# Chunked attention ahead of two expert layers: v loaded as one transfer per head, memory scored apart, q and k laid out six tokens to a partition

## The chip, the cores and the metric

One core of a Trainium2 chip runs the whole program. The metric is the device time of one execution in microseconds (us); lower is better. A run's time is that of the execution as a whole; the profile's span, from the first to the last instruction, is a little shorter.

## What is computed

Chunked attention with a few memory tokens for 4 batches and 8 heads, 768 tokens, head width 64, in float32; its output goes through a soft mixture of experts and then through a top-2 mixture of experts. Only the attention is touched:

```python
chunk, left_ctx, right_ctx = (32, 16, 8)
for c in range(nc):
    c_start = c * chunk
    c_end = c_start + chunk
    l_start = max(0, c_start - left_ctx)
    r_end = min(S, c_end + right_ctx)
    q_c = q[:, :, c_start:c_end]
    k_full = np.concatenate([mem_k, k[:, :, l_start:r_end]], axis=2)   # 8 memory tokens, up to 56 of context
    v_full = np.concatenate([mem_v, v[:, :, l_start:r_end]], axis=2)
    scores = scale * np.matmul(q_c, k_full.transpose(0, 1, 3, 2))
    a = softmax(scores)
    out[:, :, c_start:c_end] = np.matmul(a, v_full)
x = moe(out)          # soft mixture of 8 experts, 4 slots each
return moe2(x)        # top-2 mixture of 8 experts
```

## The kernel before

Attention works on units of one batch and two heads (16 units), and each unit in two halves of 12 chunks: 32 steps, counted by i or n in the code. The two heads of a unit stand on partitions 0 to 63 and 64 to 127. Tokens go in pairs of an even and an odd one (z is the parity), so that a row of 512 B in DRAM holds two tokens of one head.

- `load_raw` (L972) brings q or k of a unit on SP's DMA queue into RW, three buffers. In before, a partition gets six rows of 512 B: row p of each of the six groups of 128 token pairs.
- `tr` (L1024) makes six PE transposes (L1032) of a raw buffer into PSUM, and four ScalarE copies (L1041) bring them to QT (q, both parities interleaved) or into KB (k by head and parity). KB is KB_W wide: 20 columns for each chunk, 16 of k and 4 of memory's k.
- `fill_mem` (L1016) copies memory's k from mkT into those 4 columns of every chunk on GpSimd, four copies for a unit (in before from the loop, L1299).
- `load_v` (L983) fills one of four VB buffers with v of a half, head by head. Partition rows 0 to 15 and 20 to 31 of a head's 32 hold the context's token pairs of the 12 chunks, two transfers on SP's queue (`piece`, L992); rows 16 to 19 hold memory's v, one transfer on GpSimd's queue (L1003).
- `spread` (L1008) copies 32 partitions of VB, 768 columns, into the block for the other parity: head 0 on VectorE (L1014), head 1 on ScalarE (L1012).
- `qk` (L1045) computes a step's scores: 12 matmuls, one for each chunk, with 32 queries stationary and 4 x 32 columns of KB moving (two heads by two parities, each 28 of k and 4 of memory; the order of a head's 64 keys is free, as long as k and v have the same). Four chunks run side by side on 32 columns of the array each. A float32 matmul is two instructions in the trace.
- `mxr` and `sub` (L1068, L1074) on VectorE take the maximum and subtract it, `expo` (L1078) on ScalarE, `at` (L1083) three PE transposes, `atc` (L1089) a ScalarE copy, `av` (L1098) the product with VB, `nrm` (L1107 to L1110) the division on VectorE, `xt` and `xtc` a transpose of the result for the router's logits, `lg`, `lgc`, `lt`, `ltc` the logits.

The order is written out by hand. Step i of the loop (L1292) issues: qk(n), mxr(n) with n = i + 1, tr(i + 3), fill_mem, spread(n, 0), sub(n), expo(n), at(i), atc(i), spread(n, 1), av(i - 1), nrm(i - 1), load_v(i + 3), a weight piece in even steps (`load_piece`, 512 KB, SP's queue), the logits' parts in some steps, xt(i - 2), xtc(i - 2). Every engine runs its own instructions in this order. On VectorE, the spreading of v stands between a step's maximum and its subtraction. The last steps are spelled out in the list ORDER.

After attention, `soft` runs the first expert layer. Its weights come through the same SP queue: 16 pieces are loaded during attention, 16 into attention's buffers once these are free, the others as the layer frees buffers (`next_load`).

## Time and profile before

| | before |
|---|---|
| runs, us | 632.57 median of 3 (625.32 to 635.29) |
| the profiled execution's own time, us | 628.29 |
| its span, us | 626.5 |
| busy: PE, ACT, DVE, POOL, us | 500.8, 291.9, 332.8, 307.2 |
| DMA moved | 127.27 MB, 203 GB/s on average |
| mean granted TensorE clock | 0.926 |
| attention | about the first 185 us |

PE is TensorE, DVE VectorE, ACT ScalarE, POOL GpSimd, SP the engine that issues most transfers. The profile gives busy time by engine over stretches, waits (which engine stood still at which line, and what ended the wait), instructions in order of time, groups of instructions by line and shape, and the DMA queues with the rate over time. Averages over the whole span hide that the stages have different limits: attention and the soft layer in the first 260 us, the routing, and then the top-2 experts, where TensorE sets the end.

### The profile page before, as it was taken

Reading aid. Unit: us, or ns where it says so; the run is one execution under the profiler, and the core shown is the slowest. Engines: PE = TensorE matmul, PEld = TensorE weight load, DVE = VectorE, ACT = ScalarE, POOL = GpSimd, SP = SyncE. Lnnn points to the kernel's source line nnn. Section 1 sums busy time; section 2 is a strip of 40 time slices with the busy share of each in tenths; the row PEclk is TensorE's granted clock in tenths of the full one; section 3 lists DMA queues with packets and bytes.
Section 4 is the critical chain, followed back from the end, with each engine's and each line's share of the span. In section 5 each row is a group of like instructions: output and inputs, shape, how many; then the busy total and the mean of one; then the engine's idle time right before and its main releaser. Section 6 shows DMA issues by size and latency. Waiting matters only on the chain.

```text
span 626.5 us, 13927 instructions
## 1 busy us (share of the span) xinstructions
PE 500.8 (80%) x4667; PEld 272.6 (44%) x4667; DVE 332.8 (53%) x830; ACT 291.9 (47%) x510; POOL 307.2 (49%) x320
## 2 busy tenths in 40 slices
PE   3777767776787877437698989999999999979980
PEld 2555545554553332222353534545545445534530
DVE  5546574664776300669756475664747566452300
ACT  3867777775832110634352362634526263433310
POOL 6233333232202100069356576766758676877772
PEclk9979999888889998757898999999999999999995
DMA  9999999999999999974838779697987868435642
GB/s 149 192 204 211 189 224 181 248 194 185 219 275 374 377 410 415 290 264 169 251 41 265 181 152 237 163 248 173 235 230 184 204 156 207 80 71 95 95 57 34
DMA packets 116779, 127.27 MB, mean 203 GB/s; under 512 B 20128, under 2 KB 85300, under 8 KB 116708
## 3 DMA queue, kind: packets, MB, share of 16 engines
q1 hardware_dynamic: 97140, 109.30, 64.2%
q0 software_dynamic: 19152, 16.89, 20.2%
q8 instruction: 43, 0.70, 0.5%
q10 hardware_dynamic: 416, 0.15, 0.2%
q14 instruction: 28, 0.23, 0.1%
HBM read 94.84 MB, written 20.42 MB: 184 GB/s over the span
## 4 chain that ended last, share of the span: by engine, by line
PE 39%; DVE 6%; DMA 4%; ACT 3%; issue 2%; POOL 2%; SPq 0%; POOLq 0%; DVEq 0%; ACTq 0%
PE l L719 32%; PE l L685 3%; DMA out_dram<-y,idx 3%; PE g L340 2%; POOL out_dram L750 1%; DVE lo L695 1%; DMA C<-G 1%; ACT hi L687 1%; PE l L716 1%; DVE G L392 1%; DVE W L409 1%; ACT W L405 1%; DVE W L792 1%; ACT y L737 0%; DVE W L524 0%
## 5 line engine op out<-in xcount | busy, mean ns | idle before, releaser
L750 POOL DMA_INDIRECT out_dram<-y,idx x96 | 157.0, 1635 | 82.5 <-DMA out_dram<-y,idx 47.5
L719 PE MATMUL l<-W,hi 128*128 (+1 forms) x768 | 181.8, 391 | 0.4 <-ACT hi L687 0.4
L695 DVE SCALAR_TENSOR_TENSOR lo<-l,hi 128x1024 f16<-128x1024 f32 x49 | 59.9, 1223 | 111.8 <-ACT hi L687 97.6
L719 PEld LDWEIGHTS <-hi 128*128 128x128 f16 x768 | 75.1, 100 | 87.5 <-issue 11.8
L737 ACT ACTIVATE y<-l,gw 128x512 f32<-128x512 f32 x49 | 33.6, 685 | 155.8 <-PE l L719 76.4
L719 PE MATMUL l<-W,lo 128*128 (+1 forms) x384 | 92.5, 384 | 4.7 <-DVE lo L695 4.7
L1003 POOL DMA_DIRECT2D arena<-in_mem_v_dram x64 | 39.5, 619 | 101.2 <-PE av L1098 100.9
L644 POOL DMA_INDIRECT cg<-table,idx x49 | 52.1, 1063 | 19.9 <-issue 10.7
L719 PEld LDWEIGHTS <-lo 128*128 128x128 f16 x384 | 37.2, 99 | 49.7 <-DVE lo L695 5.5
L687 ACT ACTIVATE hi<-l 128x1024 f16<-128x1024 f32 x49 | 50.3, 1026 | 10.0 <-PE l L685 9.9
L1014 DVE COPY arena<-arena 32x768 f32<-32x768 f32 x32 | 18.1, 566 | 58.1 <-DMA arena<-in_v_dram 57.1
L409 DVE SCALAR_TENSOR_TENSOR W<-w,sc,W 128x1024 f16<-128x1024 f32 x31 | 42.3, 1390 | 0.2
L1055 PE MATMUL st<-arena,qT 128*32 128x128 f32 (+2 forms) x768 | 32.3, 309 | 12.5 <-ACT arena L1041 10.6
L1083 PE MATMUL at<-cf,a 128*128 128x128 f32 x96 | 18.2, 302 | 26.5 <-ACT aT L1089 25.4
L1032 PE MATMUL tr<-cf,arena 128*128 128x128 f32 x192 | 30.7, 300 | 10.8 <-DMA arena<-in_q_dram 9.9
L1041 ACT ACTIVATE qT<-tr 64x384 f32<-64x384 f32 x64 | 33.6, 526 | 8.6 <-PE tr L1032 7.4
L405 ACT ACTIVATE W<-w,sc 128x1024 f16<-128x1024 f32 x32 | 35.7, 1150 | 0.2
L1098 PE MATMUL av<-arena,aT 128*32 128x130 f32 x768 | 31.4, 295 | 4.4 <-issue 2.9
L1078 ACT ACTIVATE a<-a 128x384 f32<-128x384 f32 x32 | 16.7, 523 | 36.9 <-DVE a L1074 36.7
L1055 PEld LDWEIGHTS st<-arena,qT 128*32 128x32 f32 x768 | 23.5, 124 | 19.5 <-issue 16.0
L1041 ACT ACTIVATE arena<-tr 64x384 f32<-64x384 f32 x64 | 31.0, 484 | 2.1 <-PE tr L1032 1.3
L1032 PEld LDWEIGHTS tr<-cf,arena 128*128 128x128 f32 x192 | 22.4, 150 | 18.1 <-issue 10.2
(265 smaller groups left out, 678.0 us busy)
## 6 DMA issues: line engine op xcount, KB each, us to landing
w<-in_moe_w_dram SPq DMA_DIRECT2D x96, 512.0 KB
arena<-in_moe_w_dram SPq DMA_DIRECT2D x32, 512.0 KB
arena<-in_q_dram SPq DMA_DIRECT2D x16, 384.0 KB
arena<-in_k_dram SPq DMA_DIRECT2D x16, 384.0 KB
arena<-in_v_dram SPq DMA_DIRECT2D x63, 96.0 KB
out_dram<-zt SPq DMA_DIRECT2D x14, 384.0 KB
C<-G SPq DMA_DIRECT2D x21, 256.0 KB
CT<-G SPq DMA_DIRECT2D x21, 256.0 KB
```

The lines of the kernel that those rows point to most:

```text
L405: nc.scalar.activation(hi, w2, AF.Copy, scale=sc[:, rk, 5:6])
L409: stt(lo, w2, sc[:, rk, 5:6], hi, op0=OP.mult, op1=OP.subtract)
L644: nc.gpsimd.indirect_dma_start(out=CG[i], out_offset=None, in_=table, in_offset=bass.IndirectOffsetOnAxis(ap=idx[:, i:i + 1], axis=0))
L687: nc.scalar.activation(HI[i], p, AF.Relu)
L695: stt(LO[i].rearrange("p k t -> p (k t)"), p.rearrange("p k t -> p (k t)"), 0.0, HI[i].rearrange("p k t -> p (k t)"), op0=OP.max, op1=OP.s ...
L719: nc.tensor.matmul(P2[i], h[i][:, k, :], dyn(W2f, i, w * 4096 + 512 * k, 512, RG.get(i)), start=x == 0 and k == 0, stop=x == last and k == 7)
L737: nc.scalar.activation(YV[i], P2.pop(i), AF.Copy, scale=GW.pop(i))
L750: nc.gpsimd.indirect_dma_start(out=o, out_offset=bass.IndirectOffsetOnAxis(ap=idx[:, i:i + 1], axis=0), in_=y[:, DH * h:DH * h + DH], in_o ...
L1003: nc.gpsimd.dma_start(vcols(i, p + 16, 4, col, 128), bass.AP(tensor=mem_v.tensor, offset=mem_v.offset + (b * H + 2 * hp + h) * NMEM * D, a ...
L1032: nc.tensor.transpose(p[:, T, :], src[:, h, T, :], identf)
L1041: nc.scalar.activation(o, i, AF.Copy)
L1055: nc.tensor.matmul(st[32 * j:32 * j + 32, g, :, w0:w1], QT[u][:, 32 * c:32 * c + 32], kb[:, :, 20 * c + w0:20 * c + w1], start=True, stop= ...
```

## The change

For each head of a half, v's context is 28 consecutive partition rows, 0 to 27, and one transfer; memory's v goes to rows 28 to 31 (still from GpSimd's queue). The first and the last half have an edge chunk as a transfer of its own. KB holds k alone, 16 columns for each chunk; the scores of memory come from three matmuls a step with 128 queries stationary and the 16 columns of MK moving, which is filled once at the start; fill_mem and its copies are gone, and the 12 matmuls of a step move 4 x 28 columns. q and k come as six consecutive tokens (1,536 B) to a partition, in two rows; after the PE transposes the tokens are out of order, and the ScalarE copies put them in order by reading PSUM with a step of 128 elements inside a group of three.

```diff
--- before.py
+++ after.py
@@ -28,7 +28,7 @@
 F = 1024
 E = 8
 SL = 32
-KB_W = 20 * NCH + 12
+KB_W = 16 * NCH + 12
 VC = 194
 NEG = -1.0e30
 NTL = 60
@@ -958,7 +958,7 @@
     KB = [carve(4 * KB_W).rearrange("p (h z w) -> p h z w", h=2, z=2) for i in range(2)]
     RW = [carve(768).rearrange("p (h t e) -> p h t e", h=2, t=3) for i in range(3)]
     VB = [carve(NH * VC + D) for i in range(NV)]
-    mkT = carve(HP * B * NMEM).rearrange("p (c z b m) -> p c z b m", c=HP, z=2, b=B)
+    MK = carve(HP * B * 2 * NMEM).rearrange("p (c b h z m) -> p c b h z m", c=HP, b=B, h=2, z=2)
     XT = [wk.tile([128, 4, 384], F32, name=f"xT{z}", bufs=1) for z in range(2)]
     mkr = XT[0].rearrange("p j n -> p (j n)")[:H * NMEM, :B * 2 * D].rearrange("p (b z d) -> p b z d", b=B, z=2)
     one = wk.tile([128, 1], F32, name="one", bufs=1)
@@ -973,9 +973,9 @@
         u, x = divmod(n, 2)
         b, hp = divmod(u, HP)
         src = (q, k)[x]
-        nc.sync.dma_start(RW[n % 3].rearrange("p h t e -> p (h t) e"),
+        nc.sync.dma_start(RW[n % 3].rearrange("p h t e -> p h (t e)"),
                           bass.AP(tensor=src.tensor, offset=src.offset + (b * H + 2 * hp) * S * D,
-                                  ap=[[128, 128], [16384, 6], [1, 128]]))
+                                  ap=[[384, 128], [S * D, 2], [1, 384]]))
 
     def vcols(i, p, n, col, cols, c0=0, c1=NH):
         return custom(VB[i % NV][p:p + n], c0 * VC + col, [[VC, c1 - c0], [1, cols]])
@@ -994,13 +994,12 @@
                                   bass.AP(tensor=v.tensor, offset=o + first * 128 + a * 2048,
                                           ap=[[128, n], [2048, e - a], [1, 128]]))
 
-            piece(0, 16, -8, c0, NH)
+            piece(0, 28, -8, c0, c1)
             if c0:
-                piece(8, 8, 0, 0, 1)
-            piece(20, 12, 8, 0, c1)
+                piece(8, 20, 0, 0, 1)
             if c1 < NH:
-                piece(20, 8, 8, c1, NH)
-            nc.gpsimd.dma_start(vcols(i, p + 16, 4, col, 128),
+                piece(0, 24, -8, c1, NH)
+            nc.gpsimd.dma_start(vcols(i, p + 28, 4, col, 128),
                                 bass.AP(tensor=mem_v.tensor,
                                         offset=mem_v.offset + (b * H + 2 * hp + h) * NMEM * D,
                                         ap=[[128, 4], [0, NH], [1, 128]]))
@@ -1012,14 +1011,6 @@
             nc.scalar.activation(o, x, AF.Copy)
         else:
             nc.vector.tensor_copy(o, x)
-
-    def fill_mem(u, eng=nc.gpsimd):
-        b, hp = divmod(u, HP)
-        for h in range(2):
-            p = 64 * h
-            for z in range(2):
-                o = custom(KB[u % 2][p:p + 64, h, z, 16:], 0, [[20, NCH], [1, NMEM // 2]])
-                eng.tensor_copy(o, mkT[p:p + 64, hp, z, b:b + 1, :].to_broadcast([64, NCH, NMEM // 2]))
 
     def tr(n):
         u, x = divmod(n, 2)
@@ -1031,13 +1022,11 @@
             for T in range(3):
                 nc.tensor.transpose(p[:, T, :], src[:, h, T, :], identf)
             for r in range(2):
-                i = p[64 * r:64 * r + 64, :3].rearrange("p t a -> p (t a)")
+                i = custom(p[64 * r:64 * r + 64], 0, [[1, 128], [128, 3]])
                 if x == 0:
                     o = custom(QT[u][64 * h:64 * h + 64], r, [[2, 384]])
                 else:
-                    o = custom(KB[u % 2][64 * h:64 * h + 64, h, 1 - r if h == 0 else r, 8:], 0,
-                               [[20, NCH], [12, 2], [1, 8]])
-                    i = i.rearrange("p (c f a) -> p c f a", f=2, a=8)
+                    o = KB[u % 2][64 * h:64 * h + 64, h, 1 - r if h == 0 else r, 8:8 + S // 2]
                 nc.scalar.activation(o, i, AF.Copy)
         if n + 3 < 2 * NU:
             load_raw(n + 3)
@@ -1048,12 +1037,16 @@
         st = ps.tile([128, 3, 4, 32], F32, name="st", bufs=2)
         kb = KB[u % 2].rearrange("p h z w -> p (h z) w")
         for g in range(3):
+            t = 128 * (3 * s + g)
+            nc.tensor.matmul(st[:, g, :, 28:32], QT[u][:, t:t + 128], MK[:, hp, b].rearrange("p h z m -> p (h z) m"),
+                             start=True, stop=True)
+        for g in range(3):
             for j in range(4):
                 c = 12 * s + 4 * g + j
                 w0 = 8 if c == 0 else 0
-                w1 = 28 if c == NCH - 1 else 32
+                w1 = 24 if c == NCH - 1 else 28
                 nc.tensor.matmul(st[32 * j:32 * j + 32, g, :, w0:w1], QT[u][:, 32 * c:32 * c + 32],
-                                 kb[:, :, 20 * c + w0:20 * c + w1], start=True, stop=True,
+                                 kb[:, :, 16 * c + w0:16 * c + w1], start=True, stop=True,
                                  tile_position=(0, 32 * j))
         ST[i] = st
 
@@ -1062,7 +1055,7 @@
         if s == 0:
             nc.vector.memset(ST[i][0:32, 0, :, 0:8], NEG)
         else:
-            nc.vector.memset(ST[i][96:128, 2, :, 28:32], NEG)
+            nc.vector.memset(ST[i][96:128, 2, :, 24:28], NEG)
         st = ST[i].rearrange("p g (h z) w -> p (g h) (z w)", z=2)
         mx = wk.tile([128, 6], F32, name="mx")
         nc.vector.tensor_reduce(mx, st, AX.X, OP.max)
@@ -1257,6 +1250,7 @@
     nc.vector.memset(VB[0][0:32, 0:128], 0.0)
     for i in range(2):
         nc.gpsimd.memset(KB[0][64 * i:64 * i + 64, 1 - i], 0.0)
+    nc.gpsimd.memset(MK, 0.0)
     load_v(0)
     clear(0, nc.vector)
     load_raw(2)
@@ -1272,11 +1266,9 @@
         nc.tensor.transpose(p[:, b].rearrange("p c h m z -> p (c h m z)"), mkr[:, b], identf[:H * NMEM, :H * NMEM])
     for h in range(2):
         for z in range(2):
-            nc.vector.tensor_copy(mkT[64 * h:64 * h + 64, :, 1 - z if h == 0 else z].rearrange("p c b m -> p b c m"),
+            nc.vector.tensor_copy(MK[64 * h:64 * h + 64, :, :, h, 1 - z if h == 0 else z].rearrange("p c b m -> p b c m"),
                                   p[64 * h:64 * h + 64, :, :, h, :, z])
     tr(1)
-    fill_mem(0, nc.vector)
-    fill_mem(1)
     tr(2)
     load_v(2)
     nc.gpsimd.memset(one, 1.0)
@@ -1295,8 +1287,6 @@
         qk(n)
         mxr(n)
         tr(i + 3)
-        if s == 1:
-            fill_mem(u + 2)
         if i == 6:
             nc.gpsimd.dma_start(phis, phi.rearrange("(j p) s -> p j s", p=128))
         spread(n, 0)
```

## Rows read from the trace of the kernel before

**Rows 1.** Stretch, us; busy PE, PEld, DVE, ACT, POOL; clock; DMA share; GB/s.

```profile
18.00:172.00 154.00, 112.25 (x1779) 80.05 (x1774) 89.93 (x235) 114.41 (x209) 49.47 (x113) 0.92 1.11 205
```

**Rows 2.** Instructions in time: start, us, operation; exps 1, 15, 16 and 29.

```profile
18.97 0.52 ACT L1078 ACTIVATE a<-a 128x384 f32<-128x384 f32 x1 [0.48 <-DVE a L1074]
...
89.98 0.52 ACT L1078 ACTIVATE a<-a 128x384 f32<-128x384 f32 x1 [1.30 <-DVE a L1074]
93.91 0.52 ACT L1078 ACTIVATE a<-a 128x384 f32<-128x384 f32 x1
...
167.18 0.52 ACT L1078 ACTIVATE a<-a 128x384 f32<-128x384 f32 x1 [2.18 <-DVE a L1074]
```

**Rows 3.** Waits, 0 to 200 us: who waited for whom, us, times, longest.

```profile
DVE arena L1014 <- DMA arena<-in_v_dram: 57.1, 26, 4.5
ACT a L1078 <- DVE a L1074: 36.7, 24, 3.6
...
PE st L1055 <- ACT arena L1041: 10.6, 10, 1.4
```

**Rows 4.** DMA views of 2.6 to 5.6 (40 slices), 11.5 to 14.8, 185 to 195.

```profile
GB/s 26 51 142 278 306 355 340 341 341 348 355 348 348 341 355 341 348 355 348 328 335 348 355 341 321 300 287 294 294 277 345 270 249 280 287 283 294 335 290 438
...
DMA packets 791, 0.37 MB, mean 112 GB/s; under 512 B 99, under 2 KB 785, under 8 KB 791
...
DMA packets 1632, 4.10 MB, mean 410 GB/s; under 512 B 126, under 2 KB 126, under 8 KB 1630
```

**Rows 5.** DMA issues, 0 to 215 us: line, count, KB each.

```profile
w<-in_moe_w_dram SPq DMA_DIRECT2D x30, 512.0 KB
...
arena<-in_v_dram SPq DMA_DIRECT2D x63, 96.0 KB
arena<-in_v_dram SPq DMA_DIRECT2D x63, 72.0 KB
```

**Rows 6.** Groups by line, 0 to 200 us, ScalarE: busy us, mean ns | idle before.

```profile
L1041 ACT ACTIVATE qT<-tr 64x384 f32<-64x384 f32 x64 | 33.6, 526 | 8.6 <-PE tr L1032 7.4
...
L1041 ACT ACTIVATE arena<-tr 64x384 f32<-64x384 f32 x64 | 31.0, 484 | 2.1 <-PE tr L1032 1.3
...
L1012 ACT ACTIVATE arena<-arena 32x768 f32<-32x768 f32 x32 | 26.9, 842 | 2.9 <-DMA arena<-in_v_dram 2.2
...
L1078 ACT ACTIVATE a<-a 128x384 f32<-128x384 f32 x32 | 16.7, 523 | 36.9 <-DVE a L1074 36.7
L1089 ACT ACTIVATE aT<-at 128x384 f32<-128x384 f32 x32 | 15.7, 491 | 3.3 <-PE at L1083 2.6
```

**Rows 7.** The same view, VectorE's reads of PSUM.

```profile
L1068 DVE TENSOR_REDUCE mx<-st 128x6 f32<-128x384 f32 x32 | 17.9, 558 | 1.1
...
L1152 DVE TENSOR_REDUCE L<-xt 128x96 f32<-128x384 f32 x8 | 4.4, 550 | 0.3 <-PE xt L1147 0.3
```

**Rows 8.** Instructions in time on TensorE, a stretch almost without waits.

```profile
162.97 0.49 PE L1083 MATMUL at<-cf,a 128*128 128x128 f32 x3
...
163.39 0.87 PE L1098 MATMUL av<-arena,aT 128*32 128x130 f32 x24
...
164.08 0.83 PE L1135 MATMUL xt<-xT,phis 128*32 128x384 f32 x8
...
164.84 0.55 PE L1121 MATMUL xt<-cf,xs 128*128 128x128 f32 x3
...
165.32 0.86 PE L1055 MATMUL st<-arena,qT 128*32 128x128 f32 x24
...
166.11 0.87 PE L1032 MATMUL tr<-cf,arena 128*128 128x128 f32 x6
```

**Rows 9.** The same view, matmuls with 128 stationary and 32 moving columns.

```profile
197.86 1.12 PE L1241 MATMUL sm<-W,xT 128*128 128x32 f32 x8 [0.20 <-DVE W L1236]
```

**Rows 10.** The same view: the end of attention, VectorE and SP's queue.

```profile
182.19 0.55 DVE L1014 COPY arena<-arena 32x768 f32<-32x768 f32 x1 [2.19 <-DMA arena<-in_v_dram]
...
201.29 16.36 SPq L146 DMA_DIRECT2D w<-in_moe_w_dram  x16
```

## The prediction

> **What bounds the kernel now.** The stage to read is attention; the change touches nothing behind it. I read first the busy times over its steady part: from 18 to 172 us the DMA engines are busy all the time (share 1.11, packets overlapping) and yet move only 205 GB/s; ScalarE is busy 114.41 of 154 us, TensorE 112.25, VectorE 89.93, GpSimd 49.47 [rows 1]. Then the length of a step: one exp (L1078) runs per step, and from its 1st to its 29th the starts are 18.97 and 167.18, so 28 steps take 148.2 us, 5.29 us each [rows 2]. One step, from 89.98 to 93.91, took 3.93 us [rows 2]: the engines can turn faster than they do. Then the waits: VectorE stands 57.1 us in front of L1014, the spreading of v, for v's transfer; what VectorE has queued behind it, the subtraction, is then late for ScalarE's exp (36.7 us) [rows 3]. So v's landing sets the step.
>
> Why does v land late when its bytes are few? The DMA rates by stretch tell it. From 2.6 to 5.6 us, at the start, q and k are alone and run at 341 to 355 GB/s, in rows of 512 B; from 11.5 to 14.8 us mostly v and memory's v run, in rows of 512 B as well, at 112 GB/s; from 185 to 195 us weights run at 410 [rows 4]. So the row's length is not what makes v slow. It differs from q and k in that a transfer goes to 16 or to 12 partitions, not to 128. A step moves one q or k transfer (128 partitions x 6 x 512 B, 384 KB), v as 2 x (96 + 72) KB and half a weight piece of 512 KB [rows 5], memory's v (2 x 4 partitions x 12 x 512 B, 48 KB) and, on average, as much of zeros for the output. At those rates, in thousands of bytes: 393/341 = 1.15 us; (344 + 49)/112 = 3.51; 262/410 = 0.64; 49/341 = 0.14. The sum is 5.44 us against the 5.29 measured: the step is DMA time, and two thirds of it is v.
>
> **v as one transfer of 28 partitions.** Same rows and bytes, two transfers a step instead of four, 28 partitions reached at once instead of 16 and then 12. No row shows 28 partitions. Below: no gain, v stays at 112 GB/s. Above: 341, the 128-partition rate. If the rate goes with the partitions reached (14 on average gave 112), 28 give 224, and this is the row it is nearest to. Memory's v keeps its four partitions and, at 112, its 0.44 us; v's 344 KB go from 3.07 to 1.54 us. I take 1.6. The two fewer issues a step on SP, which has queued behind them only further loads, I cost at nothing: SP's queue is not what the waits name.
>
> [...]
>
> **q and k with rows of 1,536 B.** The same bytes in a third of the rows: between 341 (no gain) and 410 GB/s (weights, with longer rows) [rows 4]. I take 400, 0.98 us instead of 1.15.
>
> DMA after: 0.98 + 1.6 + 0.44 + 0.64 + 0.14 = 3.80 us a step. That is under what the engines need, so look who is next.
>
> **ScalarE.** A step has four copies of L1041 (526 ns for q, 484 for k), L1012 842, L1078 523, L1089 491: 2.02 + 1.86 = 3.88 us [rows 6], near the 3.93 of the fastest step. The change makes the four copies read PSUM with a step of 128 elements where they read it in a row. No ScalarE row shows that. The nearest is VectorE's L1152, which reads PSUM with a step of 32: 550 ns for 384 elements, against 558 for L1068 in a row [rows 7]. I cost it at nothing; it is the second rival.
>
> **TensorE.** From start to start in a stretch without waits: at 0.42, av 0.69, lg 0.76, xt 0.48, qk 0.79 us; tr, at most 0.87, about 0.70 [rows 8]. Each step has at, av, xt, qk and tr, 3.08 us; lg, and lt which is like xt, come every fourth step, 0.31 on average. The new part is three matmuls on the memory, with 128 stationary columns and 16 moving ones, in two passes each. The nearest row is L1241, 128 stationary and 32 moving: eight passes in 1.12 us, 0.14 each [rows 9]; so at most 6 x 0.14 = 0.84 us. Nothing at the least: every other step TensorE waits for k's copies ahead of qk, 10.6 us in 10 times [rows 3], and the memory's scores need only q, whose copies are a step older. I take 0.7. The narrower matmuls (112 columns for 128) give back at most an eighth of 0.79, 0.1. TensorE after: 3.08 + 0.31 + 0.7 - 0.1 = 3.99 us at full clock; granted was 0.92 on average, with more idle time than will be left [rows 1].
>
> **The rest.** fill_mem leaves GpSimd, which is idle two thirds of the stage [rows 1]; nothing. A memset of MK is put ahead of the first loads of memory's v on GpSimd, once; the first exp waits for the DMA of q's and v's first loads, which SP issues; nothing, and without that cover one memset. The new matmuls wait for the score buffer, as the first of qk did, and for q; behind them on TensorE stand qk and tr, ScalarE waits for tr; they are inside the 3.99.
>
> **The sum.** DMA 3.80, ScalarE 3.88 and TensorE 3.99 are nearly level, and each works in a fixed order and waits now and then for the others; so the step is above the largest. I take 4.3, between 3.93 and 4.7 (TensorE's 3.99 at a clock of 0.92, 4.34, and as much loss again). 28 x (5.29 - 4.3) = 27.7 us. Ahead of the first exp the same loads run: v of the first two steps, 688 KB at 112 GB/s, 6.1 us, would halve; q's third load comes late there too; I take 2 of the 3. At the end VectorE waits 2.19 us at 182.19 for the last v; I take 1. Together 30.7 us. What follows shifts along: the next 16 weight pieces are issued from 201.29 us on, when attention's end lets the first shared expert run [rows 10], not by a free DMA. The profiled execution is 628.29 us: 597.6; on the median of the runs, 632.57, it is 601.9. I say 600.
>
> **Rivals.**
> (1) v gains nothing (0.15). The packets per engine may count, not the partitions reached. Then DMA stays the bound with 5.29 - 0.17 = 5.12, 28 x 0.17 = 5 us, some 2 at the start: 621. [...] No view of the trace shows single engines.
> (2) Slower (0.06): L1041's strided read. ScalarE takes (842 - 523)/384 = 0.83 ns an element [rows 6]; a copy is 505 ns on average. ScalarE alone reaches 5.29 a step once a copy costs 505 + (5.29 - 3.88)/4 = 858 ns, twice the cost per element (825) is the edge. At three times, 1,145 ns, the step is 6.44 us: 28 x 1.15 = 32 us more, 660. Against it [rows 7]. [...]
> (3) Half (0.12): the copies get half as slow again per element (665 ns, ScalarE 4.52) or the new matmuls cost their 0.84 with the clock at 0.83, and the step ends near 4.9: 28 x 0.4 + 2 = 13 us less, 615.
> The forecast itself holds 0.67: its lower end is steps of 3.93 and all 3 + 2 us at the ends, 28 x 1.36 + 5 = 43 us less, 585 on the profile and 590 on the median, so 588; its upper end is steps of 4.7, 28 x 0.59 + 1 = 18 us less, 611 on the profile, so 612.
>
> **How the numbers follow.** About 2%, 13 us, is what a measurement here can tell. From the median, faster ends at 620. The forecast and most of (3) lie below: 0.67 + 0.11 = 0.78; (1), 625 on the median, and the rest of (3) are the same: 0.16; (2) is slower: 0.06. The range for 8 in 10 takes the forecast, (3) and, since 0.21 would be left out without it, (1) up to about its middle: 588 to 624. The forecast's own is 588 to 612.
>
> **What would show it.** Right: waits of VectorE for v's transfer near nothing; the 29 exps in about 120 us; ScalarE busy nine tenths of the stage and TensorE as much; the DMA share under 1; L1041 at 484 to 526 ns. Wrong: L1014 still waits for v with the DMA rate near 205 GB/s (rival 1); L1041 over 800 ns (rival 2); TensorE's new matmuls over 0.84 us a step, or waits of at or qk for ScalarE that grow as v's shrink.

## The result and the profile after

The changed kernel takes 613.4 us (median of 6 runs, 607.33 to 615.76), the kernel before on the same chip 632.14 (6 runs, 625.32 to 635.29): a ratio of 0.971 with an interval of 0.967 to 0.976. It is faster, by 18.7 us, inside the range of 588 to 624; but the forecast was 600, so about three fifths of the expected gain came. 613.4 also lies just outside the forecast's own 588 to 612; it is the rivals' share of the range that takes it in.

| profiled execution, us | before | after | change |
|---|---|---|---|
| time (span) | 628.29 (626.5) | 607.33 (605.5) | -21.0 |
| first exp | 18.97 | 15.22 | -3.75 |
| 29th exp | 167.18 | 144.09 | -23.1 |
| a step, mean of the 28 between | 5.29 | 4.60 | -0.69 |
| first matmul of the shared expert (L231) | 199.29 | 175.61 | -23.7 |

Both profiled executions lie below the medians of their kernels, by 4 and by 6 us; steps read from a single profile carry such a difference (6 us in 28 steps are 0.2 us a step).

The steps in time, after: start, length, operation, and in brackets how long ScalarE stood idle before it and for whom. These are the 1st, 8th, 9th and 29th exp; [rows 2] has those of before.

```profile
15.22 0.52 ACT L1071 ACTIVATE a<-a 128x384 f32<-128x384 f32 x1 [1.10 <-DVE a L1067]
...
43.41 0.52 ACT L1071 ACTIVATE a<-a 128x384 f32<-128x384 f32 x1
49.05 0.52 ACT L1071 ACTIVATE a<-a 128x384 f32<-128x384 f32 x1 [1.58 <-DVE a L1067]
...
144.09 0.52 ACT L1071 ACTIVATE a<-a 128x384 f32<-128x384 f32 x1 [2.24 <-DVE a L1067]
```

The first seven steps take (43.41 - 15.22)/7 = 4.03 us each, and after the first exp ScalarE's exp waits for nobody in them; the eighth takes 5.64. From the 9th exp to the 29th a step is 4.75. So there are two stretches, and their busy times differ (columns as in [rows 1]):

```profile
14.00:45.00 31.00, 29.22 (x470) 24.56 (x471) 21.06 (x56) 27.34 (x51) 7.92 (x13) 1.00 1.07 237
45.00:145.00 100.00, 86.52 (x1450) 68.64 (x1448) 65.45 (x172) 82.49 (x152) 25.24 (x42) 1.00 1.07 240
```

Up to 45 us TensorE is busy 94% and ScalarE 88%: the engines set the step. After that both fall (87% and 82%), at the same 1.07 of DMA share and 240 GB/s, and at a granted clock of 1.00. The DMA is the bound again, with 240 GB/s in place of 205 [rows 1]. The early steps live on what had been loaded ahead: 237 GB/s bring 955 KB in 4.03 us, and the loads of a step, added up in the prediction, are 1,097 KB; later 240 GB/s bring 1,140 KB in 4.75 us. Who waits for whom, 0 to 190 us (total, times, longest):

```profile
DVE arena L1013 <- DMA arena<-in_v_dram: 31.2, 19, 3.7
...
ACT a L1071 <- DVE a L1067: 16.8, 13, 2.4
...
PE st L1048 <- ACT arena L1030: 5.7, 12, 0.7
```

It is the same wait as before, VectorE's spread for v's transfer, shrunk from 57.1 to 31.2 us and not to nothing, and the exp's wait with it from 36.7 to 16.8 [rows 3]. The groups by line (busy us, mean ns of one) that the forecast had costed:

```profile
L1030 ACT ACTIVATE qT<-tr 64x384 f32<-64x384 f32 x64 | 33.2, 519 | 3.5 <-PE tr L1023 2.4
L1030 ACT ACTIVATE arena<-tr 64x384 f32<-64x384 f32 x64 | 30.9, 483 | 3.5 <-PE tr L1023 2.7
...
L1041 PE MATMUL st<-arena,qT 128*128 128x16 f32 x192 | 25.6, 260 | 0.0
...
L1013 DVE COPY arena<-arena 32x768 f32<-32x768 f32 x32 | 17.8, 558 | 36.5 <-DMA arena<-in_v_dram 31.2 <-issue 3.5 <-DMA arena<-in_mem_v_dram 1.5
```

ScalarE's copies (L1030), now with a step of 128 elements in PSUM, take 519 and 483 ns, where they took 526 and 484 in a row [rows 6]. The memory's matmuls keep TensorE 25.6/32 = 0.80 us a step. What follows attention shifts along as said:

```profile
175.61 1.93 PE L231 MATMUL p<-w,phis 128*32 128x256 f32 x32 [0.32 <-DVE phis L1237]
```

```profile
177.60 15.53 SPq L146 DMA_DIRECT2D w<-in_moe_w_dram  x16
```

Both are 23.7 us earlier (199.29 and 201.29 before [rows 10]). The end is 21.0 earlier; 2.7 us are lost in the last stage, where the chain that ended last goes through the scatter to the output for 8% of the span and for 3% before. One execution of each doesn't show why; that stays open.

So the question is why a step is 4.60 us and not 4.3.

### The profile page after: what moved, and what is told of

Its sections match the earlier page's. It is cut to its first block, busy times and chain, and to the rows that moved or that the text cites. A ratio compares the mean times of both kernels' runs of the same rounds, so it can differ in the third digit from the quotient of the medians.

```text
span 605.5 us, 14138 instructions
## 1 busy us (share of the span) xinstructions
PE 509.7 (84%) x4859; PEld 290.8 (48%) x4859; DVE 331.8 (55%) x826; ACT 291.5 (48%) x510; POOL 289.2 (48%) x261
## 4 chain that ended last, share of the span: by engine, by line
PE 29%; DMA 10%; DVE 6%; issue 4%; POOL 4%; ACT 4%; SPq 0%; POOLq 0%; DVEq 0%; ACTq 0%
PE l L719 25%; DMA out_dram<-y,idx 8%; PE l L685 2%; POOL out_dram L750 2%; DVE W L409 1%; POOL out_dram L745 1%; PE g L340 1%; DVE lo L695 1%; DMA C<-G 1%; ACT hi L687 1%; ACT W L405 1%; DVE W L524 1%; DMA out_dram<-y,qidx 1%; DMA w<-in_moe_w_dram 1%; ACT G L391 1%
## 5 line engine op out<-in xcount | busy, mean ns | idle before, releaser
L750 POOL DMA_INDIRECT out_dram<-y,idx x96 | 154.6, 1611 | 85.3 <-DMA out_dram<-y,idx 50.9
L1013 DVE COPY arena<-arena 32x768 f32<-32x768 f32 x32 | 17.8, 558 | 36.5 <-DMA arena<-in_v_dram 31.2
L1023 PE MATMUL tr<-cf,arena 128*128 128x128 f32 x192 | 30.7, 300 | 5.2 <-DMA arena<-in_q_dram 5.2
L1030 ACT ACTIVATE qT<-tr 64x384 f32<-64x384 f32 x64 | 33.2, 519 | 3.5 <-PE tr L1023 2.4
L1048 PE MATMUL st<-arena,qT 128*32 128x112 f32 (+2 forms) x768 | 27.5, 278 | 6.1 <-ACT arena L1030 5.7
L1030 ACT ACTIVATE arena<-tr 64x384 f32<-64x384 f32 x64 | 30.9, 483 | 3.5 <-PE tr L1023 2.7
L1091 PE MATMUL av<-arena,aT 128*32 128x130 f32 x768 | 28.6, 280 | 2.6 <-ACT aT L1082 1.4
L352 DVE TENSOR_REDUCE mxp<-w 128x1 f32<-128x2048 f32 x13 | 29.6, 2276 | 0.0
L1011 ACT ACTIVATE arena<-arena 32x768 f32<-32x768 f32 x32 | 27.0, 843 | 1.4 <-DMA arena<-in_mem_v_dram 0.5
L1041 PEld LDWEIGHTS st<-arena,qT 128*128 128x128 f32 x192 | 25.9, 205 | 0.7 <-issue 0.5
```

The lines of the kernel that those rows point to most:

```text
L352: vt(t, w2[:, part * n:(part + 1) * n], AX.X, OP.max, apply_absolute_value=True)
L750: nc.gpsimd.indirect_dma_start(out=o, out_offset=bass.IndirectOffsetOnAxis(ap=idx[:, i:i + 1], axis=0), in_=y[:, DH * h:DH * h + DH], in_o ...
L1023: nc.tensor.transpose(p[:, T, :], src[:, h, T, :], identf)
L1030: nc.scalar.activation(o, i, AF.Copy)
```

## The experiments

Three theories for the shortfall were set against each other. **A**: v's transfer with 28 partitions is hardly faster than two with 16 and 12 (the first rival). **B**: transfers slow each other down, and memory's small one costs more than its bytes. **C**: buffers come free late, so that loads start late. Later came two more: that it is the **number** of transfers in SP's queue, and that it is **GpSimd's queue** by which memory's v is issued.

### v in two transfers again (split)

```diff
-            piece(0, 28, -8, c0, c1)
+            piece(0, 16, -8, c0, c1)
+            piece(16, 12, 8, c0, c1)
```

> The changed kernel with one part undone: v of a head as two transfers again, of 16 and of 12 partitions. The prediction's sum gave the single transfer 1.5 us a step; with 28 steps bound by the DMA that is up to 30 us slower than the changed kernel, 640. Theory A: no difference, 613. Theories B and C: slower by 5 to 20 us, 618 to 633, with VectorE's waits for v back from 31 us towards the 57 of before.

Measured: 630.88 us, 1.001 of before (0.996 to 1.006). All of the gain is gone. The exp's steps are 5.26 us, and VectorE's wait is back:

```profile
DVE arena L1014 <- DMA arena<-in_v_dram: 50.4, 23, 3.5
ACT a L1072 <- DVE a L1068: 33.3, 21, 2.6
```

So the merged v is what makes the kernel faster (vhalves below tells fewer transfers from more partitions); the memory's own matmuls, the freed GpSimd and q's and k's rows bring nothing measurable without it.

### q and k in rows of 512 B again (rows512)

```diff
-        nc.sync.dma_start(RW[n % 3].rearrange("p h t e -> p h (t e)"),
+        nc.sync.dma_start(RW[n % 3].rearrange("p h t e -> p (h t) e"),
...
-                                  ap=[[384, 128], [S * D, 2], [1, 384]]))
+                                  ap=[[128, 128], [16384, 6], [1, 128]]))
...
-                i = custom(p[64 * r:64 * r + 64], 0, [[1, 128], [128, 3]])
+                i = p[64 * r:64 * r + 64, :3].rearrange("p t a -> p (t a)")
```

> The changed kernel with one part undone: q and k again as six rows of 512 B to a partition, and read in a row by ScalarE's copies. The prediction's sum gave the long rows 0.17 us a step: 618. If the fewer packets matter more than their rate alone (theory B, since they then stand less in the way of v and of weights): 5 to 12 us slower, 618 to 625. If the copies' strided read costs anything, they get shorter here than 519 and 483 ns.

Measured: 615.54 us, 0.978 (0.968 to 0.988), against 0.971 (0.967 to 0.976): the intervals overlap, so no difference is shown. The step of the profile is 4.90 where it is 4.60, but this profile lies at the median of its runs and the changed kernel's 6 us below its own. The copies now read PSUM in a row:

```profile
L1030 ACT ACTIVATE qT<-tr 64x384 f32<-64x384 f32 x64 | 33.2, 519 | 5.7 <-PE tr L1023 4.6
...
L1030 ACT ACTIVATE arena<-tr 64x384 f32<-64x384 f32 x64 | 30.9, 483 | 3.4 <-PE tr L1023 2.6
```

These are the same 519 and 483 ns to the digit. The step of 128 elements costs these copies nothing; the rival that ended on the slower side falls.

### Without memory's v (nomem)

```diff
-            nc.gpsimd.dma_start(vcols(i, p + 28, 4, col, 128),
+            if i < NV:
+              nc.gpsimd.dma_start(vcols(i, p + 28, 4, col, 128),
```

> The changed kernel with memory's v loaded for the first four steps only; the later steps use what is left there (that part of the result is left out). The prediction's sum has 0.44 us a step for it. Theories A and B: the DMA is the bound, so up to 20 steps of 0.44 us, 9 us faster, 604; more if its four partitions hold up other transfers. Theory C: no difference, 613, since v's issue is what is late.

It leaves memory's v out from the fifth step on, which changes attention's values and sends the tokens to other experts; its whole time (748.3 us) says nothing here, and only attention's steps are read. 1st, 9th and 29th exp:

```profile
16.15 0.52 ACT L1072 ACTIVATE a<-a 128x384 f32<-128x384 f32 x1 [1.42 <-DVE a L1068]
...
48.53 0.52 ACT L1072 ACTIVATE a<-a 128x384 f32<-128x384 f32 x1
...
136.00 0.52 ACT L1072 ACTIVATE a<-a 128x384 f32<-128x384 f32 x1 [1.12 <-DVE a L1068]
```

The step is 119.85/28 = 4.28 us in place of 4.60: 0.32 x 28 = 9 us for two transfers of 24 KB a step. That is about what the forecast missed in its steps (8.4 us). That 4.28 is also the 4.3 that the forecast took for a step is chance: its 4.3 had memory's v in it. Theory C expected no difference and is not borne out; A and B expected this one alike, and the loads alone have to tell them apart.

### The loads alone, in groups (probe)

At the start of the kernel, ahead of attention, groups of transfers run with no engine at work; a memset into their targets on VectorE marks the end of each group.

```diff
+    for n, p0 in ((16, 0), (12, 16), (28, 0), (32, 0), (4, 0)):
+        for j in range(6):
+            for h in range(2):
+                pv(xf, 1536 * j, h, p0, n, 0, j)
+        barrier()
```

> The changed kernel with transfers put ahead of it that nothing computes on, group after group with a memset between: v in 16, 12, 28, 32 and 4 partitions, q and k in rows of 512 and of 1,536 B, then six steps' loads at a time as the kernel before issues them, as the changed one does, the same without memory's v, and without memory's v and the weights. No buffer has to come free inside a group. Theory A, v's transfer of 28 partitions is hardly faster than those of 16 and 12: 28 alone runs at 112 to 140 GB/s. Theory B, alone it is fast (190 to 224 GB/s), but the transfers of a step slow each other: the changed kernel's mix needs 4.6 to 5.1 us a step, well over the sum of its parts. Theory C, the DMA engines could do it (28 alone at 190 to 224 GB/s, the mix in 3.6 to 4.0 us a step), and in the kernel the loads are issued late because their buffers come free late.

Twelve transfers of v (12 rows of 512 B a partition) go to 16, 12, 28, 32 and 4 partitions. The first five marks on VectorE, where each row ends a group and starts the next:

```profile
1.16 0.14 DVE L1268 MEMSET xs<- 128x96 f32 x1
...
11.74 0.14 DVE L1268 MEMSET xs<- 128x96 f32 x1 [10.33 <-DMA xs<-in_v_dram]
...
21.84 0.14 DVE L1268 MEMSET xs<- 128x96 f32 x1 [9.86 <-DMA xs<-in_v_dram]
...
33.80 0.14 DVE L1268 MEMSET xs<- 128x96 f32 x1 [11.71 <-DMA xs<-in_v_dram]
...
45.72 0.14 DVE L1268 MEMSET xs<- 128x96 f32 x1 [11.68 <-DMA xs<-in_v_dram]
```

In these stretches in the middle of the five groups the data runs all the time; the last number is GB/s:

```profile
4.00:9.50 5.50, 0.00 (x0) 0.00 (x0) 0.00 (x0) 0.00 (x0) 0.00 (x0) 1.00 1.26 155
14.00:20.00 6.00, 0.00 (x0) 0.00 (x0) 0.00 (x0) 0.00 (x0) 0.00 (x0) 1.00 0.93 111
24.00:31.50 7.50, 0.00 (x0) 0.00 (x0) 0.00 (x0) 0.00 (x0) 0.00 (x0) 1.00 1.04 224
36.00:43.50 7.50, 0.00 (x0) 0.00 (x0) 0.00 (x0) 0.00 (x0) 0.00 (x0) 1.00 1.15 256
47.00:51.50 4.50, 0.00 (x0) 0.00 (x0) 0.00 (x0) 0.00 (x0) 0.00 (x0) 1.00 0.25 59
```

The rate rises with the partitions that a transfer reaches, from 59 GB/s at 4 to 256 at 32: 28 give the 224 GB/s that the forecast scaled from 112, though 16 and 12 give 155 and 111 when they run alone. A falls. (No run shows the 190 GB/s at the lower end of what B and C expected.) From mark to mark the groups of 16, 12 and 28 take 10.58, 10.10 and 11.96 us. Of each group some 2.2 us, an estimate (by the rates 2.1 to 3.0), are the marks, the way to the first data and the last landing. Without these, v of a step costs alone 2.71 us in two pieces and 1.63 in one; by the rates above, 2.6 and 1.54. So the forecast had v's new price right (1.6) and its old one too high (3.07).

The groups behind that were not clean: memory's v of the next group, issued by GpSimd, ran ahead into them. Hence the second one, below.

### Memory's v from on-chip memory (onchip)

```diff
-            nc.gpsimd.dma_start(vcols(i, p + 28, 4, col, 128),
-                                bass.AP(tensor=mem_v.tensor,
...
+            nc.gpsimd.tensor_copy(vcols(i, p, 4, col, 128), MV[p:p + 4, u % 8:u % 8 + 1, :].to_broadcast([4, NH, 128]))
...
+        if i in (7, 15):
+            load_mv(u + 5, 4, nc.gpsimd)
```

MV holds memory's v of eight head pairs and is loaded with six transfers in all; GpSimd, idle here without memory's transfers (0.00 us busy in memsp, 45 to 145 us), copies it into place. To suit its partitions, memory's four rows go ahead of the context's 28 (scores' columns 0 to 3, v's rows 0 to 3).

> The changed kernel without memory's transfers: memory's v of eight units lies once in the chip's memory, GpSimd copies it into each buffer's 12 chunks (rows 0 to 3 of 32, v in rows 4 to 31), two copies a step. In the loads without buffers the mix took 4.27 us a step with memory's v and 3.53 without. If memory's v holds the other transfers up (theory B), the steps 8 to 28 go from 4.75 to about 4.3, near the engines' 4.0, and the run to 598 to 606. If the DMA isn't what binds there (theory C), or GpSimd's copies, some 1.6 us each, come late or hold VectorE up: no better than 613.

Measured: 605.67 us, 0.955 (0.942 to 0.967); the interval just meets the changed kernel's (0.967 to 0.976). Steps: 4.56 us in the profile, 4.64 from the 9th on, where about 4.3 was expected. The profile of the changed kernel has 4.60 and 4.75, so the 7.7 us between the medians do not show in these two profiles' steps.

```profile
L1009 POOL COPY arena<-arena 4x1536 f32<-4x1536 f32 x64 | 96.3, 1504 | 43.7 <-PE av L1098 32.8 <-DVE a L1074 4.3 <-DMA arena<-in_mem_v_dram 4.0
...
L1020 DVE COPY arena<-arena 32x768 f32<-32x768 f32 x32 | 25.5, 798 | 19.6 <-DMA arena<-in_v_dram 18.7 <-POOL arena L1009 0.2
```

VectorE's wait for v falls to 18.7 us. Part of the gain goes to a new cost: beside GpSimd's copies (1,504 ns for four partitions) VectorE's spread takes 798 ns in place of 558, 0.24 us a step; without such copies it took 551 to 566 ns (before, split, rows512, memsp, vhalves), with them 755 in onchip_nz and 865 in split_onchip.

### And the zeros moved out of attention (onchip_nz)

```diff
-            if i in (8, 12):
-                x = (8, 12).index(i)
-                zero_out(nc.sync, out, zt, x * 100 // 8, (x + 1) * 100 // 8)
...
-    for x in range(2, 8):
+    for x in range(0, 8):
```

> As onchip, and the two lots of zeros for the output, which are issued in attention with weight pieces 8 and 12, are issued after the soft layer with the others. Without memory's loads one step of 6.98 us stood among steps of 4.0 to 4.4, where zeros are issued. If they are the cause: 3 to 5 us faster than onchip, 594 to 602, unless what they move to has no room for them: then no gain, with a later table or first expert tile.

Measured: 599.86 us (598.45 to 603.94), 0.950 (0.941 to 0.959): faster than both kernels. First and 29th exp:

```profile
16.18 0.52 ACT L1075 ACTIVATE a<-a 128x384 f32<-128x384 f32 x1 [1.43 <-DVE a L1071]
...
137.94 0.52 ACT L1075 ACTIVATE a<-a 128x384 f32<-128x384 f32 x1 [0.18 <-DVE a L1071]
```

The step is 4.35 in place of onchip's 4.56: 5.9 us in 28 steps, and 5.8 lie between the medians. The two intervals overlap, so it is onchip and this edit together that are shown to beat the changed kernel, and how much of that is memory's v and how much the zeros is not shown.

### Memory's v by SP's queue (memsp)

```diff
-            nc.gpsimd.dma_start(vcols(i, p + 28, 4, col, 128),
+            nc.sync.dma_start(vcols(i, p + 28, 4, col, 128),
```

> The changed kernel with memory's v issued on SP's queue instead of GpSimd's, same rows and partitions. If GpSimd's queue (its descriptors, its packets between the others) is what costs: like onchip, 600 to 607. [...]

Measured: 621.89 us, 0.983 (0.975 to 0.991); the step is 5.09. The interval just meets the changed kernel's (0.967 to 0.976), but its fastest run, 620.16, is above that kernel's slowest, 615.76.

```profile
DVE arena L1013 <- DMA arena<-in_mem_v_dram: 40.3, 21, 4.5
ACT a L1071 <- DVE a L1067: 25.5, 15, 3.5
```

Now memory's v is what lands last. Taking it off GpSimd's queue does not make it cheap. Whether it is dearer here because it stands in SP's order behind other loads, no run shows.

### The loads alone, cleanly (probe2)

The same groups with a mark that also holds back GpSimd's queue; six steps' loads to a group.

```diff
+    for wide, pieces, mem, w in ((1, (), 0, 0), (1, (), 1, 0), (None, (28,), 1, 0), (0, (16, 12), 1, 1), (1, (28,), 1, 1),
+                                 (1, (28,), 0, 1), (1, (16, 12), 1, 1), (0, (28,), 1, 1)):
```

> The changed kernel again with transfers ahead of it that nothing computes on, each group of six steps' loads closed off on all queues: long q and k rows alone; these with memory's v; v in 28 partitions with memory's v; then whole steps with weights: as before, as changed, as changed without memory's v, and as changed with one part undone (v in 16 and 12; rows of 512 B). In the first such run memory's v of the before mix had run in the group ahead of it, beside the long rows alone, which then took 13.9 us instead of some 8. If the contention theory (B) holds: long rows alone 7.5 to 8.5 us a group, with memory's v 12 to 14; memory's v worth 0.6 to 0.9 us a step in the changed mix; the mix before 5.1 to 5.5 us a step, changed 4.2 to 4.4, with v in two 5.0 to 5.4 (the kernel's steps hardly gained there), rows of 512 B 4.4 to 4.7. If the kernel's steps come from buffers that free late (C): v in two below 4.9 and the mix before below 5.0, under the 5.26 and 5.45 us that the kernels' later steps take.

The marks on VectorE; each of these rows ends a group, and the first starts group A:

```profile
1.27 0.14 DVE L1269 MEMSET xs<- 128x96 f32 x1
...
11.19 0.14 DVE L1269 MEMSET xs<- 128x96 f32 x1
...
27.03 0.14 DVE L1269 MEMSET xs<- 128x96 f32 x1 [0.56 <-DMA xs<-in_mem_v_dram]
...
41.82 0.14 DVE L1269 MEMSET xs<- 128x96 f32 x1 [14.31 <-DMA xs<-in_mem_v_dram]
...
72.48 0.14 DVE L1269 MEMSET xs<- 128x96 f32 x1 [1.02 <-DMA xs<-in_v_dram]
...
101.44 0.14 DVE L1269 MEMSET xs<- 128x96 f32 x1 [0.60 <-DMA xs<-in_v_dram]
...
124.32 0.14 DVE L1269 MEMSET xs<- 128x96 f32 x1 [0.46 <-issue]
...
154.62 0.14 DVE L1269 MEMSET xs<- 128x96 f32 x1 [1.12 <-DMA xs<-in_v_dram]
...
182.74 0.14 DVE L1269 MEMSET xs<- 128x96 f32 x1 [1.34 <-DMA xs<-in_v_dram]
```

| group | mark to mark | a step, (us - 2.2)/6 |
|---|---|---|
| A: q or k, rows of 1,536 B | 9.92 | 1.29 |
| B: A and memory's v | 15.84 | 2.27 |
| C: v in one and memory's v | 14.79 | 2.10 |
| D: before's mix (512 B rows, v in two, memory's v, weights) | 30.66 | 4.74 |
| E: the changed mix | 28.96 | 4.46 |
| F: E without memory's v | 22.88 | 3.45 |
| G: E with v in two | 30.30 | 4.68 |
| H: E with 512 B rows | 28.12 | 4.32 |

A and H also hold loads of the kernel's own start (0.15 and 0.07 MB), and A starts slowly. In B the last of q and k itself lands later than in A:

```profile
11.05 0.11 DVE L1268 MEMSET arena<- 128x64 f32 x1 [9.54 <-DMA arena<-in_k_dram]
...
26.36 0.11 DVE L1268 MEMSET arena<- 128x64 f32 x1 [14.92 <-DMA arena<-in_k_dram]
```

So memory's v holds others up: 5.4 us for its six steps here. It costs 4.46 - 3.45 = 1.01 us a step in the mix and 0.98 beside q and k alone (B - A), where its bytes were costed at 0.44; beside v alone it costs less, 2.10 - 1.63 = 0.47. In the mix it takes a twentieth of the step's bytes and over a fifth of its time. (GpSimd issued all twelve of its transfers within 11.2 us in group B and 7.3 in group C; in the kernel they are spread over the steps.) With the zeros' 0.14, E is 4.60, the changed kernel's mean step, and 0.15 under its steps after the ninth exp (4.75): by this reckoning, good to some 0.1 us, these are almost nothing but loads, and theory C, buffers that come free late, has 0.15 us a step there. Without memory's v the loads would be down at 3.45 + 0.14 = 3.59, under the engines' 4.03, and then the engines would set most steps (nomem's first eight take 4.05); so nomem gains 0.32 and not 1.01.

Long rows of q and k bring nothing in the mix (E with 28.96 us is no shorter than H with 28.12). Alone they do run faster, if not over the whole of A. These are the rates in 40 slices, first rows of 512 B (53.6 to 63.2 us of the first such run), then A (1.3 to 11.2 us):

```profile
GB/s 0 0 0 0 81 124 79 139 245 350 346 346 344 346 352 339 318 326 341 348 350 346 346 346 348 346 339 352 348 348 344 346 346 346 314 218 30 0 0 0
...
GB/s 0 16 119 184 13 57 254 72 50 279 379 385 379 354 372 385 379 404 403 379 335 267 211 285 354 397 366 372 397 397 397 403 391 310 192 124 62 6 0 0
```

One thing doesn't fit, and it bears on theory C. By G, v in two pieces costs 0.22 us a step more than in one, in the kernel 0.66 (split); and D with the zeros is 4.88, the kernel before 5.29. The expectation had named such values, v in two below 4.9 (it is 4.68) and the mix before below 5.0 (4.74), as the sign that buffers come free late; B's values for them, 5.0 to 5.4 and 5.1 to 5.5, were missed. So for the two kernels with v in pieces the loads alone leave 0.4 us a step or more unexplained, and theory C is not ruled out there.

### More transfers without fewer partitions (vhalves, rawtwo)

Is it the number of transfers, and what SP waits for between them? v in two halves by its chunks, 28 partitions each, and q or k in two transfers by head:

```diff
-            piece(0, 28, -8, c0, c1)
+            piece(0, 28, -8, c0, 6)
+            piece(0, 28, -8, 6, c1)
```

> The changed kernel with v of a head as two transfers of 28 partitions, six chunks each: the same rows, partitions and bytes, but four transfers of v a step, as before. Theory P, the partitions that a transfer reaches make the gain: like the changed kernel, 610 to 617. Theory N, the number of transfers makes it (in the kernel with v in 16 and 12, SP stood some 75 us in wait for earlier transfers to land, in the changed one some 12): like that kernel, 624 to 634, with those waits of SP back.

```diff
-        nc.sync.dma_start(RW[n % 3].rearrange("p h t e -> p h (t e)"),
...
+        for h in range(2):
+            nc.sync.dma_start(RW[n % 3][:, h].rearrange("p t e -> p (t e)"),
+                              bass.AP(tensor=src.tensor, offset=src.offset + (b * H + 2 * hp + h) * S * D,
+                                      ap=[[384, 128], [1, 384]]))
```

> The changed kernel with q and k as two transfers, one for each head, instead of one: the same rows of 1,536 B, partitions and bytes, one transfer a step more on SP. Theory P: like the changed kernel, 610 to 617. Theory N: between that and the kernel with v in two, 616 to 626, with SP in wait for earlier transfers for 20 to 50 us.

Measured: vhalves 612.78 us (four runs: three of 612.7 to 613.34 and one of 602.04, too far apart for an interval), rawtwo 609.85, 0.972 (0.962 to 0.981); steps of 4.69 in both. No run of either is above 613.4, the changed kernel's median. SP's queue does wait much more with v in halves. What SP stood for ahead of v's issues, 15 to 165 us, first vhalves, then the changed kernel:

```profile
SPq L993 <- DMA arena<-in_k_dram: 19.0, 14, 1.9
SPq L993 <- DMA arena<-in_q_dram: 11.3, 9, 1.8
SPq L993 <- DMA w<-in_moe_w_dram: 10.1, 10, 1.6
```

```profile
SPq L993 <- PE av L1091: 16.5, 17, 2.1
...
SPq L993 <- DMA arena<-in_v_dram: 4.5, 9, 1.2
```

It waits for earlier loads to land, where in the changed kernel it waits for buffers to come free; and the time does not grow by it. More transfers alone do not bring back what split lost (612.78 and 609.85 against 630.88), so in this kernel it is the partitions of a transfer that count, and SP's queue is not a bound.

### v in two without memory's transfers (split_onchip)

```diff
-            piece(4, 28, -8, c0, c1)
+            piece(4, 16, -8, c0, c1)
+            piece(20, 12, 8, c0, c1)
```

This is onchip with v in two.

> onchip (memory's v copied by GpSimd, no transfers for it) with v of a head again as two transfers, of 16 and of 12 partitions. With memory's transfers, v in two cost 17 us; in the loads alone it cost only 0.23 us a step, 6 us. If v in two is slow by itself: 17 us over onchip's 606 again, 618 to 626, the steps 5.1 or more. If it is slow only beside memory's transfers: 606 to 613, the steps 4.6 to 4.8.

Measured: 612.1 us, 0.970 (0.961 to 0.979), against 605.67, 0.955 (0.942 to 0.967), for onchip: 6.4 us between the medians, 9.7 by the ratios, with intervals that overlap. The step is 4.83 against 4.56, but this profile is the slowest of its five runs (618.33 us). With memory's transfers running, the same cut costs 17.5 us (630.88 to 613.4) and 0.66 a step, and there the intervals lie far apart.

```profile
DVE arena L1021 <- DMA arena<-in_v_dram: 21.3, 14, 2.5
```

So v in two pieces seems to be dear mainly where memory's small transfers run beside it; the medians say so, the intervals leave room for the opposite. By what mechanism is not settled: the loads alone, with memory's v among them, did not show the excess (G against E), so something of the running kernel belongs to it, as when a load is let go. No run took that apart.

## Side by side

The ratio is to runs of the kernel before on the same chip (their medians lie between 629.69 and 632.88), so medians of different rows compare less well than ratios. Steps are from one profile each: 1st to 9th exp, 9th to 29th, and all 28.

| kernel | median, us | ratio to before | first exp | steps: early, later, all |
|---|---|---|---|---|
| before | 632.14 | 1 | 18.97 | 4.89, 5.45, 5.29 |
| changed | 613.4 | 0.971 (0.967 to 0.976) | 15.22 | 4.23, 4.75, 4.60 |
| split | 630.88 | 1.001 (0.996 to 1.006) | 18.39 | 5.23, 5.27, 5.26 |
| rows512 | 615.54 | 0.978 (0.968 to 0.988) | 16.32 | 4.50, 5.06, 4.90 |
| nomem | not comparable | | 16.15 | 4.05, 4.37, 4.28 |
| memsp | 621.89 | 0.983 (0.975 to 0.991) | 16.88 | 4.56, 5.30, 5.09 |
| onchip | 605.67 | 0.955 (0.942 to 0.967) | 16.10 | 4.35, 4.64, 4.56 |
| onchip_nz | 599.86 | 0.950 (0.941 to 0.959) | 16.18 | 4.04, 4.47, 4.35 |
| split_onchip | 612.1 | 0.970 (0.961 to 0.979) | 17.52 | 4.67, 4.89, 4.83 |

## Why the prediction was right, and where it fell short

**What bounds the kernel: right.** v's landing set the step; with v cut up again the gain is gone (split). But that the old sum, 5.44, met the 5.29 measured was luck in part: measured one by one its parts are 393/344 = 1.14, 2.71, 1.01, 0.64 and 0.14, together 5.64, and issued together they take 4.88 (D and the zeros).

**v at 28 partitions: the rate right, the gain too high.** 224 GB/s measured, 224 forecast; 1.54 to 1.63 us a step alone, 1.6 forecast. Its old price was put too high, 3.07 for 2.71. The 112 GB/s of [rows 4] came from a stretch where v and memory's v ran together, and all of it was charged to the bytes of both alike; 16 and 12 partitions alone run at 155 and 111, so that 224, scaled from 112, came out to the digit is chance. Merging v was to save 1.5 us of DMA time a step; it saves 1.08 alone, 0.22 in the loads of a step together, and 0.66 in the kernel.

The charge on both alike is also what failed. **The step that failed is memory's v: "at 112, its 0.44 us".** Measured in the mix it is 1.01. Per byte it is the dearest load of the stage (1.01 us for 49,000 bytes; v alone, in one piece, 1.63 for 344,000), and it was costed like v. With 1.01 for 0.44 the sum of the DMA is 4.37 in place of 3.80, above TensorE's 3.99; the changed loads together, with the zeros, take 4.60. So the DMA stays the bound of the steady steps, and the forecast's picture, engines level and the DMA just under them, came only in the first seven. The forecast's own way of bounding it, one rate for v and memory's v, had no room for this: the upper end of its price would have been to charge the excess of the slow stretch to memory's v.

**q and k in long rows: the rate right, the gain not shown.** Alone they run at 354 to 404 GB/s over most of A, with a dip to 211, where short rows run at 344; 400 was forecast. In the mix they bring nothing (E and H), and in the kernel the medians differ by 2 us with overlapping intervals.

**ScalarE and TensorE: right.** The copies cost what they did; the memory's matmuls keep TensorE 0.80 us, between the bounds of 0 and 0.84 and near the 0.7 taken. The first seven steps, 4.03 us, are the engines' floor that was worked out as 3.99. The floor was there; the loads reached it only while buffers had been filled ahead. The granted clock was 1.00 (14 to 145 us), not 0.92.

**SP's fewer issues and fill_mem at nothing: right.** More issues on SP again cost nothing that shows (vhalves 612.78 and rawtwo 609.85, against 613.4), and GpSimd was busy 33 of 131 us (14 to 145 us).

**The signs it named.** Of the five for right, L1041's 484 to 526 ns came (519 and 483). The waits for v near nothing did not (31.2 us), nor the DMA share under 1 (1.07); the 29 exps took 129 us for 120, and ScalarE and TensorE were busy about nine tenths or more only up to 45 us.

**The sum.** Steps 28 x 0.69 = 19.3 us for 27.7; the start 3.75 for 2; attention's tail 0.6 for 1; the last stage -2.7 for 0. Together 21.0 for 30.7. The steps carry 8.4 of the 9.7 that are missing, and nomem, by one profile, gains 9.

**The range.** The forecast's upper end, 611 on the profile, is 615 on the median by the step that put its lower end from 585 to 590; 612 was too low for its own sum. That 613.4 fell into 588 to 624 is owed in part to what the rivals added, and none of their causes showed.

**The rivals.** The first (v gains nothing, by the packets per engine) falls: alone, the groups of 16 and 12 partitions took 10.58 and 10.10 us, 20.68 together, and 28 at once 11.96; in the kernel v in two costs 17.5 us (split). What a single engine does, no view shows, so whether its packets count as well is not shown. The second (ScalarE's strided reads) falls by rows512. The third (half the gain, 615) named the time well and the wrong causes: copies and matmuls were as forecast.

## What to carry to other kernels

When a stretch runs at a low rate, find out which of the transfers in it is slow before pricing all of them at that rate: two loads of 24 KB into four partitions cost a step more than twice what their bytes were priced at (1.01 us for 0.44). Where a small operand is loaded anew in every step, try to keep it on chip and copy it with an idle engine (here 7.7 us between medians whose intervals meet), and look whether that engine slows a neighbour (here VectorE's copies, from 558 to 798 ns). Give a transfer as many partitions as the layout allows: 28 at once in place of 16 and then 12 was worth 17.5 us in this kernel.

## What the runs showed that was not expected

- Two transfers of 24 KB into four partitions each, rows of 512 B, lengthen a step of loads by 1.01 us (4.46 and 3.45). Alone, transfers to four partitions moved 59 GB/s with a DMA share of 0.25, by which these 49,000 bytes take 0.83 us: in the mix they cost all of that and more, though they are a twentieth of the bytes. Why is not shown; beside v alone they cost 0.47.
- The kernel was slower when SP's queue issued memory's v than when GpSimd's did (621.89 and 613.4 us).
- In onchip GpSimd's copies of 4 x 1,536 elements took 1,504 ns, and VectorE's copies in SBUF grew from 558 to 798 ns on average.
- ScalarE reads 384 fp32 elements from PSUM with a step of 128 elements in the time that it takes for a row of them (519 and 483 ns both ways, after and rows512).
